# Normalising the first batch's probabilities inside the transposition: a float32 product with a diagonal of reciprocal sums in place of a POOL multiplication

## The chip, the cores and the metric

The kernel runs on one core of a Trainium2 chip. The metric is the device time of one execution in microseconds (us). The engines are named as the profile names them: PE (TensorE matrix products), PEld (its weight loads), DVE (VectorE), ACT (ScalarE), POOL (GpSimd), SP (the engine that starts the loads from memory).

## What is computed

Causal attention with a window of 128 positions and a distance bias, over 8 batches, 8 heads, 576 positions and 64 columns a head; then one feed-forward network over all 4608 rows.

```python
scores = scale * np.matmul(q, k.transpose(0, 1, 3, 2))
...
scores = np.where(mask, scores + bias[None], -1000000000.0)
scores = scores - np.max(scores, axis=-1, keepdims=True)
attn = np.exp(scores)
attn = attn / (np.sum(attn, axis=-1, keepdims=True) + 1e-09)
x = np.matmul(attn, v)            # heads laid side by side: 4608 x 512
...
h = x @ w_in                      # 512 x 2048
g = h * (1.0 / (1.0 + np.exp(-1.702 * h)))
out = g @ w_out                   # 2048 x 512
```

## The kernel before

Attention is done in units: one or two blocks of 128 (or 64) query rows, each against the 128 keys before it and its own. A unit goes through stages, one stage a tick, so that four units are under way at once: `scores` (PE, into `s_ps`, of which there is one buffer), `biased` (DVE adds the bias and takes the row minimum of the negated scores), `exponents` (ACT, with the row sum), `normal` (reciprocal of the sums on DVE, then the multiplication of the probabilities `b.p`, tile `pb`), `flip` (PE transposes the probabilities into `t_ps`, two buffers, which the decoding of weights uses too), `high` (ACT copies them to SBUF, tile `pw` or `ph`), `mix` (PE multiplies by V into `x_ps`), and the copy of the result into `x0` or `xf`, the rows that the network takes.

The first batch is treated otherwise than the rest. Its units are *whole* (`u.whole`): their products with Q, K and V are in plain float32, and their probabilities are multiplied by the reciprocal sums on POOL (L345). There are 24 of them, eight (one a head) for each of the row ranges 0 to 256, 256 to 512 and 512 to 576, called the first, second and third part below. A unit of the first part has two blocks and 3 transposed pieces of 128x128, one of the second two blocks and 4 pieces, one of the third one block of 64 rows and 2 pieces with 64 output columns: 24 + 32 + 16 = 72 pieces. The later batches split every operand into a high and a low float32r part and are normalised on DVE (L349) or ACT (L347); the change does not touch them.

The network works in chunks of 256 rows. For each of the 16 slices `f` of the hidden layer, `up` issues 12 products of 256 columns into `h_ps` (L452), ACT, DVE and POOL form the gate and split it (L457, L458, L461, L462), and `down` issues 6 products of 512 columns into `acc` (L471). The first chunk needs the rows of the first part alone. The weights arrive as raw words and are decoded once, by two operations on ACT (L219, L220), two on DVE (L221, L222), a cast on ACT (L224) and a subtraction on POOL (L225). While the first part is prepared, three products that nobody reads (L197, `spin`) stand behind each tick on PE.

The code issues all this in one program order, ticks between the network's steps by a running credit. A scheduler then orders each engine's instructions by its own estimate of durations; each engine works its list in that order. The loads on SP keep the order of the program. A load of Q or K for a later unit needs one of three raw buffers back, and so waits for the scores of an earlier unit; loads of weights stand behind them on the same queue.

Of the kernel before, what the change touches and what calls it, by code (L numbers as in the profile page):

```python
# [8 lines left out]
F32 = mybir.dt.float32  # L9
# [6 lines left out]
ALU = mybir.AluOpType  # L16
# [5 lines left out]
P = 128  # L22
# [135 lines left out]
def tile_kernel(ctx: ExitStack, tc: tile.TileContext, qT, kT, v, w_in, w_out, out):  # L158
    nc = tc.nc
# [3 lines left out]
    att = ctx.enter_context(tc.tile_pool(name="att", bufs=2))  # L163
# [10 lines left out]
    ident = const.tile([P, P], F32, name="ident")  # L174
# [162 lines left out]
    def normal(u, on_act):  # L337
        u.rec = att.tile([P, 2], F32, name="rec", bufs=3)
        rows, ne = u.blocks[0].rows, len(u.blocks)
        nc.vector.tensor_scalar(u.rec[:rows, :ne], u.sums[:rows, :ne], 1e-9, None, ALU.add)  # L340
        nc.vector.reciprocal(u.rec[:rows, :ne], u.rec[:rows, :ne])
        for e, b in enumerate(u.blocks):
            live = b.p[:rows, b.live:b.end]
            if u.whole:
                nc.gpsimd.tensor_scalar(live, live, u.rec[:rows, e:e + 1], None, ALU.mult)  # L345
            elif on_act:
                nc.scalar.activation(live, live, AF.Copy, scale=u.rec[:rows, e:e + 1])  # L347
            else:
                nc.vector.tensor_scalar(live, live, u.rec[:rows, e:e + 1], None, ALU.mult)  # L349

    def flip(u):

        u.t = ps.tile([P, 4 * P], F32, name="t_ps", bufs=2)
        if u.whole:
            u.ph = u.pl = att.tile([P, 4 * P], F32, name="pw", tag="ph")
        else:
            u.ph = att.tile([P, 4 * P], F32R, name="ph")
            u.pl = att.tile([P, 4 * P], F32R, name="pl")
        u.pspans = []
        w = 0  # L360
        for c in u.chunks:
            start = w
            for b, col in c.parts:
                nc.tensor.transpose(  # L364
                    u.t[:c.n, w:w + b.rows], b.p[:b.rows, col:col + c.n], ident[:b.rows, :b.rows])
                w += b.rows
            c.p = u.ph[:c.n, start:w], u.pl[:c.n, start:w]
            if u.pspans and u.pspans[-1][0] == c.n:
                u.pspans[-1][2] = w
            else:  # L370
                u.pspans.append([c.n, start, w])
# [124 lines left out]
    for b in range(1, B):  # L496
        start = (b * S + S - 1) // T - XBUFS
# [12 lines left out]
    def tick():  # L510

        nonlocal ticks
        n = ticks

        def stage(k, *steps):
            u = units[n + k] if 0 <= n + k < len(units) else None
            for step in steps:
                if u:
                    step(u)

        stage(1, split_q)
        stage(-2, flip, split_v)
        stage(0, lambda u: None if u.whole else load_v(u))
        stage(-1, lambda u: load_v(u) if u.whole else None)
        stage(-1, biased)
        stage(1, split_rest)
        stage(-1, exponents)
        on_act = n - 1 in BESIDE
        if on_act:
            stage(-2, high)  # L530
        stage(-1, lambda u: normal(u, on_act))
        if not on_act:
            stage(-2, high)
        stage(-2, low)
        stage(0, scores)
        stage(-3, mix)
        if n + 1 < len(units) and units[n + 1] and loads:
            load(loads.pop(0))
        ticks += 1
# [121 lines left out]
```

## Time and profile before

| | us |
|---|---|
| median of 3 runs | 1069.25 (1067.49 to 1070.32) |
| the profiled execution | 1072.22 |
| its span, first to last instruction | 1070.4 |
| PE busy over the span | 1054.6 (99%) |
| DVE, ACT, POOL busy | 706.7, 605.4, 636.1 |

The profiled execution took 3.0 us more than the median. Busy time of PE is modelled from overlapping instructions; a PE that is 99% busy says that it hardly ever waits, not that it works at its peak. The first batch's units lie in the first 130 us of the span; from there to the end PE works the network and the later batches. The rows on which the prediction rests stand in it.

### The profile page before, as it was taken

Reading aid. Unit: us, or ns where it says so; the run is one execution under the profiler, and the core shown is the slowest. Engines: PE = TensorE matmul, PEld = TensorE weight load, DVE = VectorE, ACT = ScalarE, POOL = GpSimd, SP = SyncE. Lnnn points to the kernel's source line nnn. Section 1 sums busy time; section 2 is a strip of 40 time slices with the busy share of each in tenths; the row PEclk is TensorE's granted clock in tenths of the full one; section 3 lists DMA queues with packets and bytes.
Section 4 is the critical chain, followed back from the end, with each engine's and each line's share of the span. In section 5 each row is a group of like instructions: output and inputs, shape, how many; then the busy total and the mean of one; then the engine's idle time right before and its main releaser. Section 6 shows DMA issues by size and latency. Waiting matters only on the chain.

```text
span 1070.4 us, 21794 instructions
## 1 busy us (share of the span) xinstructions
PE 1054.6 (99%) x7021; PEld 941.6 (88%) x7021; DVE 706.7 (66%) x2299; ACT 605.4 (57%) x1797; POOL 636.1 (59%) x931
## 2 busy tenths in 40 slices
PE   7999999999999999999999999999999999999998
PEld 4676899998989999999999999999999999998987
DVE  4767898879897777654676668767867687413131
ACT  4797776676766566444555556656565556322222
POOL 3679986667776666544565657656666566323232
PEclk9799999999999999999999999999999999999999
DMA  4974322333322232202222212222222121000000
GB/s 136 305 235 145 83 63 86 105 84 86 86 79 80 60 88 77 61 12 67 63 71 66 62 52 86 72 69 67 85 67 85 52 68 51 9 12 21 1 21 20
DMA packets 97265, 81.24 MB, mean 76 GB/s; under 512 B 50048, under 2 KB 88448, under 8 KB 97152
## 3 DMA queue, kind: packets, MB, share of 16 engines
q1 hardware_dynamic: 91968, 70.42, 23.4%
q10 hardware_dynamic: 5184, 9.44, 2.4%
q8 instruction: 55, 0.90, 0.3%
q14 instruction: 58, 0.48, 0.1%
HBM read 70.39 MB, written 9.44 MB: 75 GB/s over the span
## 4 chain that ended last, share of the span: by engine, by line
PE 93%; DVE 3%; ACT 2%; DMA 1%; issue 1%; POOL 0%; SPq 0%; DVEq 0%; POOLq 0%; ACTq 0%
PE h_ps L452 37%; PE acc L471 37%; PE x_ps L398 5%; PE t_ps L364 5%; PE s_ps L309 5%; PE s_ps L303 1%; PE x_ps L393 1%; PE acc L197 1%; DMA rk<-kT 1%; DMA rw<-w_in 1%; DVE pb L321 1%; ACT pb L332 0%; ACT rw L220 0%; DVE xh L436 0%; SPq L170 0%
## 5 line engine op out<-in xcount | busy, mean ns | idle before, releaser
L452 PE MATMUL h_ps<-xh,w 128*128 128x256 f32 x2304 | 370.1, 284 | 3.6 <-DVE g L458 2.1
L462 POOL TENSOR_TENSOR gl<-g,gh 128x256 fp32r<-128x256 f32 x288 | 215.7, 750 | 255.8 <-ACT gh L461 194.4
L452 PEld LDWEIGHTS h_ps<-xh,w 128*128 128x128 f32 x2304 | 328.2, 188 | 34.7 <-DVE g L458 3.4
L471 PE MATMUL acc<-w,gh 128*128 128x512 f32 x1152 | 325.5, 399 | 0.0
L458 DVE SCALAR_TENSOR_TENSOR g<-g,h_ps 128x256 f32<-128x256 f32 x288 | 119.4, 415 | 180.5 <-ACT g L457 178.9
L457 ACT ACTIVATE g<-h_ps 128x256 f32<-128x256 f32 x288 | 109.6, 381 | 204.1 <-PE h_ps L452 182.5
L471 PEld LDWEIGHTS acc<-w,gh 128*128 128x128 f32 x1152 | 196.0, 188 | 26.9 <-ACT pw L375 0.6
L461 ACT CAST gh<-g 128x256 fp32r<-128x256 f32 x288 | 116.9, 406 | 141.3 <-DVE g L458 129.3
L452 PE MATMUL h_ps<-xl,w 128*128 128x256 f32 x1152 | 194.6, 280 | 0.0
L471 PE MATMUL acc<-w,gl 128*128 128x512 f32 x576 | 188.1, 401 | 0.0
L332 ACT ACTIVATE pb<-pb,mins 128x256 f32<-128x256 f32 (+3 forms) x292 | 141.4, 486 | 58.7 <-DVE mins L321 55.0
L296 POOL TENSOR_TENSOR K<-rk,K 128x384 fp32r<-128x384 f32 (+1 forms) x140 | 126.8, 906 | 77.7 <-ACT Q L276 22.5
L452 PEld LDWEIGHTS h_ps<-xl,w 128*128 128x128 f32 x1152 | 163.3, 188 | 5.5
L321 DVE CUSTOM_DVE_ANT_0 pb<-s_ps,bias 128x256 f32<-128x256 f32 (+5 forms) x320 | 114.6, 377 | 25.3 <-PE s_ps L303 15.5
L295 POOL TENSOR_TENSOR Q<-rq,Q 64x256 fp32r<-64x256 f32 (+1 forms) x140 | 96.4, 689 | 25.3 <-ACT Q L276 5.7
L349 DVE TENSOR_SCALAR pb<-pb,rec 128x256 f32<-128x256 f32 (+2 forms) x252 | 108.5, 467 | 3.3
L364 PE MATMUL t_ps<-ident,pb 128*128 128x128 f32 (+1 forms) x548 | 100.7, 275 | 1.2 <-DVE pl L381 0.6
L471 PEld LDWEIGHTS acc<-w,gl 128*128 128x128 f32 x576 | 92.4, 188 | 8.2 <-POOL pb L345 0.5
L340 DVE TENSOR_SCALAR rec<-sums 128x2 f32<-128x2 f32 (+2 forms) x164 | 51.1, 312 | 61.3 <-ACT pb L332 60.0
L309 PE MATMUL s_ps<-K,Q 128*128 128x256 f32 (+1 forms) x504 | 91.5, 290 | 0.0
L381 DVE TENSOR_TENSOR pl<-t_ps,ph 128x512 fp32r<-128x512 f32 (+2 forms) x140 | 84.1, 603 | 5.4 <-ACT ph L375 5.1
L294 DVE CAST K<-rk 128x384 fp32r<-128x384 f32 (+1 forms) x140 | 57.5, 411 | 34.2 <-PE s_ps L309 30.2
(56 smaller groups left out, 1277.2 us busy)
## 6 DMA issues: line engine op xcount, KB each, us to landing
rk<-kT SPq DMA_DIRECT2D x84, 192.0 KB, 2.6
rq<-qT SPq DMA_DIRECT2D x112, 128.0 KB, 2.5
out<-o ACTq DMA_DIRECT2D x36, 256.0 KB, 2.3
rw<-w_in SPq DMA_DIRECT2D x16, 512.0 KB, 5.2
rw<-w_out SPq DMA_DIRECT2D x16, 512.0 KB, 6.4
rk<-kT SPq DMA_DIRECT2D x56, 128.0 KB, 2.3
rv<-v SPq DMA_DIRECT2D x100, 64.0 KB, 1.9
rq<-qT SPq DMA_DIRECT2D x44, 64.0 KB, 2.2
```

The lines of the kernel that those rows point to most:

```text
L296: nc.gpsimd.tensor_tensor(K2, rk, K1.bitcast(F32), ALU.subtract)
L309: nc.tensor.matmul(u.s[:b.rows, e, b.first:b.end], u.Q[:, b.q0 - u.q0:b.q0 - u.q0 + b.rows], k[:, ko:ko + b.end - b.first], start=(z == 0) ...
L321: nc.vector.tensor_tensor_reduce(b.p[ra:rb, cs:b.end], u.s[ra:rb, e, cs:b.end], bias[head][ra:rb, cs:b.end], -SCALE, BIG, ALU.add, ALU.min ...
L332: nc.scalar.activation(live, live, AF.Exp, bias=u.mins[:b.rows, e:e + 1], scale=-1.0, accum_out=u.sums[:b.rows, e:e + 1],)
L349: nc.vector.tensor_scalar(live, live, u.rec[:rows, e:e + 1], None, ALU.mult)
L364: nc.tensor.transpose(u.t[:c.n, w:w + b.rows], b.p[:b.rows, col:col + c.n], ident[:b.rows, :b.rows])
L452: nc.tensor.matmul(h, w1[f][:, z, k * P:(k + 1) * P], x[:, k], start=(n == 0), stop=(n == len(ops) - 1))
L457: nc.scalar.activation(g, h, AF.Tanh, scale=0.851)
L458: nc.vector.scalar_tensor_tensor(g, g, 1.0, h, ALU.add, ALU.mult)
L461: nc.scalar.copy(gh, g)
L462: nc.gpsimd.tensor_tensor(gl, g, gh.bitcast(F32), ALU.subtract)
L471: nc.tensor.matmul(acc, g[:, t * P:(t + 1) * P], w2[f][:, z], start=(f == self.f0 and n == 0), stop=(f == self.f1 - 1 and n == 2))
```

## The change

For whole units, `normal` no longer multiplies the probabilities on POOL. DVE multiplies the 128x128 identity (64x64 in the third part) by a block's column of reciprocal sums instead, which gives a diagonal matrix, `b.scale`, in a tile that takes its room from the tag `pl` (two buffers; whole units have no `pl` of their own). `flip` then replaces each transposition by a float32 product of the probabilities with that diagonal: the same stationary operand, another moving one, the result transposed and normalised at once. All other units keep their code.

```diff
+        if u.whole:
+            u.scale = att.tile([P, 4 * P], F32, name="scale", tag="pl")
         for e, b in enumerate(u.blocks):
             live = b.p[:rows, b.live:b.end]
             if u.whole:
-                nc.gpsimd.tensor_scalar(live, live, u.rec[:rows, e:e + 1], None, ALU.mult)
+                b.scale = u.scale[:rows, e * P:e * P + rows]
+                nc.vector.tensor_scalar(
+                    b.scale, ident[:rows, :rows], u.rec[:rows, e:e + 1], None, ALU.mult)
...
             for b, col in c.parts:
-                nc.tensor.transpose(
-                    u.t[:c.n, w:w + b.rows], b.p[:b.rows, col:col + c.n], ident[:b.rows, :b.rows])
+                p, to = b.p[:b.rows, col:col + c.n], u.t[:c.n, w:w + b.rows]
+                if u.whole:
+                    nc.tensor.matmul(to, p, b.scale, start=True, stop=True)
+                else:
+                    nc.tensor.transpose(to, p, ident[:b.rows, :b.rows])
```

Line numbers behind `flip` are 7 higher after the change (L452 is L459, L471 is L478, L393 is L400). The scheduler also orders the engines anew, up to the second batch; SP's order stays as it was. Three places matter below.

The first is PE in the first part, at the first two units' transpositions. `t_ps<-ident` is a transposition, `t_ps<-scale` the product in its place, `s_ps` the scores of the fourth unit (u3), `x_ps` the first unit's product with V. Before:

```order
L364 MATMUL t_ps_184<-ident_73,pb_162 128x128
L364 MATMUL t_ps_184<-ident_73,pb_164 128x128 x2
L303 MATMUL s_ps_236<-rk_153,rq_152 128x128
L303 MATMUL s_ps_236<-rk_153,rq_152 128x256
L364 MATMUL t_ps_215<-ident_73,pb_192 128x128
L393 MATMUL x_ps_239<-pw_185,VV_159 64x256
```

and now:

```order
L370 MATMUL t_ps_185<-scale_172,pb_162 128x128
L370 MATMUL t_ps_185<-scale_172,pb_164 128x128 x2
L370 MATMUL t_ps_217<-scale_203,pb_193 128x128
L370 MATMUL t_ps_217<-scale_203,pb_195 128x128 x2
L303 MATMUL s_ps_239<-rk_153,rq_152 128x128
L303 MATMUL s_ps_239<-rk_153,rq_152 128x256
```

Three pieces stood ahead of u3's scores and six products stand there now.

The second is POOL between the first part and the network's first steps, where its multiplications stood among the decoding of weights (`w1`, `w2`, L225) and the splitting of the gate (`gl`, L462). Before:

```order
L345 TENSOR_SCALAR pb_512<-pb_512,rec_520 128x256
L345 TENSOR_SCALAR pb_514<-pb_514,rec_520 128x256
L345 TENSOR_SCALAR pb_648<-pb_648,rec_656 128x256
L345 TENSOR_SCALAR pb_650<-pb_650,rec_656 128x256
L225 TENSOR_TENSOR w1_1_583<-wc_578,w1_1_583 128x512
L225 TENSOR_TENSOR w2_1_592<-wc_587,w2_1_592 128x512
L462 TENSOR_TENSOR gl_570<-g_566,gh_569 128x256
L225 TENSOR_TENSOR w1_2_605<-wc_600,w1_2_605 128x512
```

and now:

```order
L445 TENSOR_TENSOR xl_554<-x0_245,xh_553 128x256
L225 TENSOR_TENSOR w1_1_593<-wc_588,w1_1_593 128x512
L225 TENSOR_TENSOR w2_1_602<-wc_597,w2_1_602 128x512
L225 TENSOR_TENSOR w1_2_615<-wc_610,w1_2_615 128x512
L225 TENSOR_TENSOR w2_2_624<-wc_619,w2_2_624 128x512
L469 TENSOR_TENSOR gl_580<-g_576,gh_579 128x256
```

The decoding of the second pair of weights has nothing of the attention ahead of it any more.

The third is PE in the second part, where transpositions stand among the network's products. Before:

```order
L471 MATMUL acc1_695<-w2_2_614,gh_808 128x512
L364 MATMUL t_ps_724<-ident_73,pb_648 128x128 x2
L364 MATMUL t_ps_724<-ident_73,pb_650 128x128 x2
L364 MATMUL t_ps_758<-ident_73,pb_733 128x128 x2
L364 MATMUL t_ps_758<-ident_73,pb_735 128x128 x2
L471 MATMUL acc0_694<-w2_2_614,gl_809 128x512
```

and now:

```order
L459 MATMUL h_ps_1005<-xh_553,w1_4_723 128x256 x4
L370 MATMUL t_ps_770<-scale_755,pb_744 128x128 x2
L370 MATMUL t_ps_770<-scale_755,pb_746 128x128 x2
L303 MATMUL s_ps_793<-rk_543,rq_542 128x256 x2
L459 MATMUL h_ps_1005<-xh_553,w1_4_723 128x256 x4
```

The pieces stay in PE's list, four to a unit, between products of the network and scores.

## Prediction

> **What bounds the kernel now.** I read the page's busy times and the engines' shares of the chain that ended last, then busy times by stage, then the chain in order of time through the first 130 us, and last the groups of the instructions that the change touches. The page first: busy time of each engine, and the chain's shares.
>
> ```profile
> PE 1054.6 (99%) x7021; PEld 941.6 (88%) x7021; DVE 706.7 (66%) x2299; ACT 605.4 (57%) x1797; POOL 636.1 (59%) x931
> ...
> PE 93%; DVE 3%; ACT 2%; DMA 1%; issue 1%; POOL 0%; SPq 0%; DVEq 0%; POOLq 0%; ACTq 0%
> ```
>
> PE carries the chain, POOL none of it. So a microsecond added to PE where PE is the bound arrives at the end whole, and POOL's time counts only where PE waits for it. Where that is, the stretches of the first batch tell (stretch, length, then busy us of PE, PEld, DVE, ACT, POOL, then granted clock, DMA share, GB/s):
>
> ```profile
> 0.00:24.00 24.00, 19.37 (x102) 12.12 (x102) 9.21 (x47) 8.56 (x28) 9.97 (x20) 1.00 0.42 113
> 24.00:42.00 18.00, 16.71 (x59) 10.19 (x59) 10.99 (x36) 12.22 (x34) 9.56 (x11) 0.62 0.92 280
> 42.00:54.00 12.00, 10.82 (x66) 8.05 (x64) 10.60 (x27) 12.00 (x27) 9.51 (x9) 1.00 1.01 354
> 54.00:105.00 51.00, 48.30 (x276) 35.13 (x276) 35.53 (x115) 44.69 (x115) 42.92 (x45) 1.00 0.64 196
> 105.00:130.00 25.00, 25.00 (x160) 20.49 (x160) 20.63 (x58) 19.04 (x60) 22.84 (x29) 1.00 0.25 67
> ```
>
> Four regimes: to 24 us nothing is full; from 24 to 42 PE is nearly full at a granted clock of 0.62; from 42 to 54 ACT is full (12.00 of 12) with the decoding of weights; from 54 on PE is full but for 2.7 us. The chain in order of time (start, length, what) says what ends each:
>
> ```profile
> 15.80 0.85 PE s_ps L303 x4
> 16.65 0.27 PE t_ps L364
> ...
> 17.84 5.46 DMA rw<-w_in
> 23.37 0.62 ACT w_ps L219
> ...
> 24.57 0.36 ACT pw L375
> ...
> 32.77 0.43 PE t_ps L364 x2
> 33.20 2.00 PE s_ps L303 x4
> ...
> 55.02 1.06 PE s_ps L303 x4
> ...
> 60.74 0.87 PE t_ps L364 x8
> ...
> 65.67 1.01 PE x_ps L393 x6
> ...
> 86.43 0.26 PE t_ps L364 x2
> ...
> 93.26 0.51 PE x_ps L393 x4
> ```
>
> Until 23.4 us everything stands behind the first load of weights: ACT has its decoding (L219) ahead of the copy `pw`, and PE needs that copy.
>
> **The change part by part.** *A product against a transposition.* A float32 product is two records (the scores of the first two parts have 24 products of 256 columns, which show as x48):
>
> ```profile
> L303 PE MATMUL s_ps<-rk,rq 64*128 64x256 f32 x48 | 15.2, 427 | 0.2 <-DVE mins L321 0.2
> ```
>
> A transposition is one. Eight transpositions of 128 columns took 0.87 us, 0.109 each. The nearest products: two of 256 columns (L303 x4) took 1.06 us, so 0.53 each; V's three (L393 x6, of 128, 256 and 128 columns) took 1.01 us, so one of 128 is (1.01 - 0.53) / 2 = 0.24 us. The first part's scores, 128 and 256 columns, took 0.85 us, which would leave 0.32 for the short one, with a weight load in it that nothing hid. Bounds: 0.22 (two transpositions) and 0.32; I take 0.24, since those products follow one another as the new ones will. That is +0.13 us a piece at full clock (bounds 0.11 and 0.21). In the third part two pieces of 64 columns took 0.26 us, two products of 64 columns (L393 x4) 0.51: +0.25 a unit. In all PE gets 56 x 0.13 + 8 x 0.25 = 9.3 us more. What of it reaches the end, by stage:
>
> - To 24 us (12 pieces): the load of `w_in` was issued at 17.84, behind loads that wait for the fifth unit's scores, which ended at 16.65. The new order puts six products (1.44 us) ahead of the fourth unit's scores where three pieces stood; 1.44 - 0.33 = 1.1 us more, of which the wait for DVE's row minima hides about half, so these scores come some 0.6 us later; the fifth unit's come only about 0.2 later, because the pieces that stood between the two have gone ahead. Taken: +0.2 (0 to 0.6).
> - 24 to 42 us (12 pieces, 9 of them at half clock by the timeline): there a piece took 0.43 / 2 = 0.215, twice as much, so a product adds 0.26: 9 x 0.26 + 3 x 0.13 = 2.7 us. PE is on the chain around 33 us, but ACT (12.2 of 18 us) and the DMA (0.92) follow closely, and the exchange of POOL's latency for DVE's shortens the way to the pieces. Taken: +1.5 (0 to 2.7).
> - 42 to 54 us (4 pieces, 0.5 us): PE is idle 1.2 us, ACT is the bound. Taken 0; with that cover gone, 0.5.
> - 54 us on (28 pieces and the 8 units of the third part): 28 x 0.13 + 2.0 = 5.6 us. PE idles 2.7 us here, of which 1.6 is one wait that no transposition is near (below). I let 1 us be filled. Taken: +4.6 (3 to 8, the upper end at 0.21 a piece).
>
> *POOL's multiplications go.* Groups by form (line, engine, operation, shapes, count, then busy us and mean ns):
>
> ```profile
> L345 POOL TENSOR_SCALAR pb<-pb,rec 128x256 f32<-128x256 f32 x24 | 22.1, 929 | 7.7 <-DVE rec L341 4.7 <-ACT w_ps L219 2.3 <-ACT w L224 0.8
> L345 POOL TENSOR_SCALAR pb<-pb,rec 64x192 f32<-64x192 f32 x8 | 6.3, 795 | 0.2 <-DVE rec L341 0.2
> L345 POOL TENSOR_SCALAR pb<-pb,rec 128x128 f32<-128x128 f32 x8 | 4.8, 602 | 17.7 <-DVE rec L341 16.1 <-ACT pb L332 1.0 <-DVE rec L340 0.6
> ```
>
> That is 33.2 us off POOL, which was 84% busy from 54 to 105. What PE waited for there and at 49 us (waits of PE and PEld: for whom, total us, times, longest):
>
> ```profile
> PE h_ps L452 <- POOL w L225: 1.1, 1, 1.1
> PE h_ps L452 <- DVE g L458: 1.6, 1, 1.6
> PEld acc L471 <- POOL pb L345: 0.5, 2, 0.3
> PEld t_ps L364 <- POOL w L225: 0.4, 1, 0.4
> ```
>
> The 1.1 us fell at 49, where POOL subtracted the decoded weights behind two multiplications; but ACT was full there, so at most half counts. With the 0.5, I take -1.0 for all of this (0 to -2.0).
>
> *DVE gets 40 diagonals.* No row shows one. The multiplication of the other batches on DVE, in the same shape, bounds it from above, an operation on one column from below:
>
> ```profile
> L349 DVE TENSOR_SCALAR pb<-pb,rec 128x128 f32<-128x128 f32 x28 | 12.1, 433 | 0.7
> L340 DVE TENSOR_SCALAR rec<-sums 64x1 f32<-64x1 f32 x8 | 1.1, 142 | 0.9 <-ACT pb L332 0.8
> ```
>
> Between 0.14 and 0.43; the same shape is the near one, so 0.43 and 17 us on DVE in all. Two of them (0.86) still come sooner than two multiplications on POOL (1.86). They queue ahead of the next unit's bias, on which its scores wait, and in the ACT stage DVE is at 10.60 of 12. Elsewhere DVE has a third of its time free. Taken: +0.3 (0 to 6, which is the third rival). The room of tag `pl` is not used by whole units, and SP's order is unchanged, so neither costs anything; if the room were short, a diagonal would wait for an earlier unit's products.
>
> Sum: 0.2 + 1.5 + 0 + 4.6 - 1.0 + 0.3 = 5.6 us. From about 140 us on the orders are those of before, and PE is the bound, so nothing makes up for it later. Against the profiled execution of 1072.2 this is 1077.8; that execution stands 3.0 above the median, so against the median of 1069.25 it is 1074.9, and I say 1075.
>
> **The rivals.** *The clock comes back sooner.* The granted clock (the seventh number) was lost after PE had stood still:
>
> ```profile
> 23.00:24.00 1.00, 0.00 (x0) 0.00 (x0) 0.00 (x0) 0.63 (x2) 0.00 (x0) 1.00 0.96 196
> 24.00:25.00 1.00, 0.02 (x1) 0.02 (x1) 0.40 (x1) 1.00 (x3) 0.00 (x0) 0.58 0.92 302
> ...
> 36.00:37.00 1.00, 1.00 (x5) 0.51 (x4) 0.29 (x1) 0.97 (x3) 0.95 (x2) 0.50 0.25 66
> 37.00:38.00 1.00, 1.00 (x5) 0.66 (x3) 0.45 (x2) 0.00 (x0) 0.55 (x1) 0.59 0.69 168
> ```
>
> Half clock from about 24.2 to 37.8, 13.6 us, although PE was busy nearly throughout. With PE fuller, half speed could end earlier or never begin. Each microsecond less of it saves half of one on PE, 6.8 in all, but ACT was idle only 18 - 12.2 = 5.8 us there. Saved 5 of it, the time is 1070: no change. Against it: the wait that brought it on, behind the load of weights, remains. [...]
>
> *POOL was what PE's late inputs hung on (not slower).* POOL was 84% busy from 54 to 105 and stands between the gate's two halves (L462), so units come late in ways that the waits put down to others. The loads of weights on PE show it as short stops from 54 to 130:
>
> ```profile
> PEld x_ps L393 <- issue: 1.6, 6, 0.4
> PEld h_ps L452 <- issue: 1.3, 5, 0.3
> PEld t_ps L364 <- issue: 1.3, 4, 0.4
> PEld s_ps L303 <- issue: 1.0, 5, 0.4
> ```
>
> These 5.2 us and the 2.7 us of idle PE make 7.9. If POOL's relief frees all of it, 5.6 us of new products fit in and 2.3 are won: 0.2 + 1.5 - 2.3 - 1.0 = -1.6, or 1067.7. It decides once more than some 6 us of the 7.9 hang on POOL; the waits that name POOL come to 2.0 in all, which is against it.
>
> *The diagonals come late.* DVE operations that should take 0.3 us took 1.2 beside POOL's subtractions of weights, as the timeline shows:
>
> ```profile
> 27.95 1.27 POOL L225 TENSOR_TENSOR w<-wc,w 128x512 fp32r<-128x512 f32 x1
> ...
> 28.14 1.23 DVE L436 CAST xh<-x 128x256 fp32r<-128x256 f32 x1
> ...
> 38.02 0.29 DVE L436 CAST xh<-x 128x256 fp32r<-128x256 f32 x1
> ```
>
> A diagonal is an operation of the same kind. If one in three of the 16 second- and third-part units is held by 1 us and PE has nothing else in its order, that is 5 to 6 us more: 1081. [...]
>
> **How the numbers follow.** A measurement of this kernel can tell about 0.3%, 3.2 us. The forecast, has 0.60. Its bounds add up to 3 - 2 = 1 and 0.6 + 2.7 + 0.5 + 8 + 0.3 = 12.1 us; all ends of one side will hardly meet, so its own range is 1071 to 1080. Of the others, the clock has 0.14, POOL 0.13, the late diagonals 0.13. The range reaches into the rivals' times on both sides: 1067 to 1081. Slower: 0.52 of the forecast's 0.60 and all of the last, 0.65. Faster by 3.2 us needs two of the gains together, or the clock's with little cost: 0.11. The rest, 0.24, is within.
>
> **What would show it.** Right: L370 as two records a product, 144 in all, and four products at about 0.96 us in the chain; no L345 on POOL, which falls by 33 us; the stage that ended at 54 at nearly the same time, and the rest 4 to 6 us later. The `w_in` load near 18.0. Wrong: products at 0.2 us or less a piece; a granted clock of 1.00 before 34 us; PE's short stops gone from 54 to 105; or PE waiting for L348. The weakest step is how much of the new PE work idle time swallows.

## The result and the profile after

The changed kernel takes 1084.16 us (median of 4 runs, 1078.42 to 1084.92) where the kernel before took 1069.78 beside it (4 runs): a ratio of 1.0116, 95% interval 1.0076 to 1.0156. A second measurement gave 1082.77 (6 runs, 1081.41 to 1086.57) against 1070.05 (17 runs): 1.0126, 1.0085 to 1.0166. The forecast was 1075, its range ended at 1081. It is slower, as forecast, but by 12 to 14 us and not by 5.6.

In the expectations and below, "after" is the changed kernel, and a gain or loss "by the ratio" is the ratio of the runs times 1070 us.

The page of the profiled execution (1084.52 us), busy times and then the chain's shares:

```profile
PE 1064.7 (98%) x7093; PEld 952.3 (88%) x7093; DVE 722.7 (67%) x2339; ACT 607.4 (56%) x1797; POOL 604.4 (56%) x891
...
PE 91%; DVE 5%; ACT 1%; issue 1%; DMA 1%; POOL 0%; SPq 0%; DVEq 0%; POOLq 0%; ACTq 0%
```

POOL fell by 31.7 us, DVE rose by 16.0 and PE by 10.1, with 72 records more. The span rose by 12.3 (1070.4 to 1082.7). So PE's idle time, span less busy, did not fall: 15.8 us before, 18.0 now. This subtraction is the reading that the rest hangs on.

Busy times by stretch, in the columns of the prediction's table, with one more row:

```profile
0.00:24.00 24.00, 20.31 (x119) 13.70 (x120) 12.55 (x62) 10.52 (x32) 2.53 (x10) 1.00 0.46 129
24.00:42.00 18.00, 16.53 (x71) 11.08 (x71) 12.21 (x41) 11.29 (x31) 3.27 (x3) 0.72 0.79 254
42.00:54.00 12.00, 8.50 (x50) 6.38 (x49) 11.26 (x30) 10.84 (x26) 5.04 (x4) 0.96 0.98 345
54.00:105.00 51.00, 50.55 (x292) 38.54 (x291) 36.70 (x112) 40.66 (x99) 24.33 (x24) 0.98 0.60 187
105.00:130.00 25.00, 24.21 (x147) 19.19 (x146) 20.08 (x51) 17.12 (x50) 19.28 (x23) 1.00 0.28 76
130.00:160.00 30.00, 28.48 (x194) 25.02 (x193) 28.01 (x81) 21.47 (x63) 23.99 (x32) 1.00 0.23 63
```

The last row of these in the kernel before:

```profile
130.00:160.00 30.00, 30.00 (x211) 27.57 (x211) 27.50 (x87) 21.37 (x63) 25.44 (x35) 1.00 0.28 74
```

PE's idle time per stretch is length less busy. From 54 to 105 us it fell from 2.70 to 0.45: the products fill it. From 42 to 54 it rose from 1.18 to 3.50, and between 105 and 160, where PE was full before, 0.79 + 1.52 = 2.31 us are new. In the last stretch DVE is at 28.01 of 30.

The chain in order of time (start, length, what) shows the place at 42 to 54 and the price of the products:

```profile
11.65 1.34 PE t_ps L370 x12
...
17.10 4.35 DMA rw<-w_in
...
41.94 4.25 DMA rw<-w_out
...
50.70 0.67 DVE wc L222
51.36 0.80 DVE scale L348 x2
52.17 0.61 DVE w_ps L221
52.77 0.33 DVE g L465
53.10 0.04 issue
53.15 2.93 PE h_ps L459 x12
56.08 1.14 PE t_ps L370 x8
...
63.89 0.89 PE t_ps L370 x8
...
114.11 0.62 PE t_ps L370 x4
```

In the list of PE's waits from 42 to 54 us it is one wait (for whom, total us, times, longest):

```profile
PE h_ps L459 <- DVE g L465: 3.0, 1, 3.0
```

PE stands for 3.0 us, from 50.16 on, before the network's products `h_ps`, which need the buffer that DVE's gate step `g` gives back. For the first 1.2 us ACT's part of the gate (L464) was not done, since ACT works on decoding ahead of it; for the rest DVE is not at `g` yet, behind decoding (L221, L222) and two diagonals. The timeline of POOL, DVE and ACT there (start, length, operation, what it waited for):

```profile
48.49 1.27 POOL L225 TENSOR_TENSOR w<-wc,w 128x512 fp32r<-128x512 f32 x1 [3.64 <-ACT w L224]
48.90 0.89 DVE L340 TENSOR_SCALAR rec<-sums 128x2 f32<-128x2 f32 x1
...
50.62 1.27 POOL L225 TENSOR_TENSOR w<-wc,w 128x512 fp32r<-128x512 f32 x1 [0.86 <-ACT w L224]
51.01 0.64 ACT L464 ACTIVATE g<-h_ps 128x256 f32<-128x256 f32 x2
51.29 0.68 DVE L348 TENSOR_SCALAR scale<-ident,rec 128x128 f32<-128x128 f32 x1
...
52.69 0.73 DVE L465 SCALAR_TENSOR_TENSOR g<-g,h_ps 128x256 f32<-128x256 f32 x2
```

Two operations of DVE took longer than usual and ended with a subtraction of POOL: `rec` 0.89 us, where the median of the first 130 us is 0.16, and the first of the two diagonals 0.68, where the median of all 40 is 0.28. Together that is 1.1 us. In the kernel before, `g` stood right behind DVE's copy into `xf`, with no decoding between:

```profile
48.03 0.41 DVE L427 COPY xf<-x_ps 64x256 f32<-64x256 f32 x1
48.36 0.40 DVE L458 SCALAR_TENSOR_TENSOR g<-g,h_ps 128x256 f32<-128x256 f32 x1
```

Now that copy (L434) starts at 50.38, and L222, the diagonals and L221 stand between it and `g`. When PE goes on, it is at half clock:

```profile
50.00:51.00 1.00, 0.15 (x2) 0.00 (x0) 1.00 (x4) 1.00 (x3) 0.38 (x1) 1.00 1.02 397
...
53.00:54.00 1.00, 0.85 (x4) 0.85 (x5) 1.00 (x4) 1.00 (x4) 1.00 (x1) 0.53 1.01 406
54.00:55.00 1.00, 1.00 (x6) 1.00 (x6) 0.90 (x3) 1.00 (x3) 1.00 (x3) 0.50 0.99 389
```

### The profile page after: what moved, and what is told of

Read it like the earlier page. It is cut to its first block, busy times and chain, and to the rows that moved or that the text cites. A ratio compares the mean times of both kernels' runs of the same rounds, so it can differ in the third digit from the quotient of the medians.

```text
span 1082.7 us, 21916 instructions
## 1 busy us (share of the span) xinstructions
PE 1064.7 (98%) x7093; PEld 952.3 (88%) x7093; DVE 722.7 (67%) x2339; ACT 607.4 (56%) x1797; POOL 604.4 (56%) x891
## 3 DMA queue, kind: packets, MB, share of 16 engines
q1 hardware_dynamic: 91968, 70.42, 22.9%
## 4 chain that ended last, share of the span: by engine, by line
PE 91%; DVE 5%; ACT 1%; issue 1%; DMA 1%; POOL 0%; SPq 0%; DVEq 0%; POOLq 0%; ACTq 0%
PE h_ps L459 36%; PE acc L478 36%; PE x_ps L405 5%; PE s_ps L309 5%; PE t_ps L372 4%; PE t_ps L370 2%; PE s_ps L303 1%; PE x_ps L400 1%; PE acc L197 1%; DVE pb L321 1%; DVE w_ps L221 1%; DVE xh L443 0%; DVE pb L353 0%; DVE wc L222 0%; DVE g L465 0%
## 5 line engine op out<-in xcount | busy, mean ns | idle before, releaser
L459 PE MATMUL h_ps<-xh,w 128*128 128x256 f32 x2304 | 370.6, 284 | 6.7 <-DVE g L465 4.6
L459 PEld LDWEIGHTS h_ps<-xh,w 128*128 128x128 f32 x2304 | 328.3, 189 | 36.6 <-DVE g L465 6.8
L478 PE MATMUL acc<-w,gh 128*128 128x512 f32 x1152 | 325.8, 400 | 0.7 <-ACT gh L468 0.7
L464 ACT ACTIVATE g<-h_ps 128x256 f32<-128x256 f32 x288 | 109.7, 382 | 204.1 <-PE h_ps L459 189.0
L478 PEld LDWEIGHTS acc<-w,gh 128*128 128x128 f32 x1152 | 195.8, 188 | 27.8 <-ACT gh L468 1.2
L459 PE MATMUL h_ps<-xl,w 128*128 128x256 f32 x1152 | 196.0, 281 | 0.0
L478 PE MATMUL acc<-w,gl 128*128 128x512 f32 x576 | 188.2, 401 | 0.0
L459 PEld LDWEIGHTS h_ps<-xl,w 128*128 128x128 f32 x1152 | 164.3, 188 | 6.0 <-DVE xl L445 0.2
L478 PEld LDWEIGHTS acc<-w,gl 128*128 128x128 f32 x576 | 92.7, 188 | 8.8 <-issue 0.8
L372 PE MATMUL t_ps<-ident,pb 128*128 128x128 f32 x476 | 87.0, 273 | 1.2 <-DVE pl L388 0.6
```

What stands on the lines that cost most here:

```text
L372: nc.tensor.transpose(to, p, ident[:b.rows, :b.rows])
L459: nc.tensor.matmul(h, w1[f][:, z, k * P:(k + 1) * P], x[:, k], start=(n == 0), stop=(n == len(ops) - 1))
L464: nc.scalar.activation(g, h, AF.Tanh, scale=0.851)
L478: nc.tensor.matmul(acc, g[:, t * P:(t + 1) * P], w2[f][:, z], start=(f == self.f0 and n == 0), stop=(f == self.f1 - 1 and n == 2))
```

## The experiments

The first four do a part of the change, or a variant of it, in the order that the scheduler then makes. The next seven hold an order fixed: the instructions are edited in each engine's finished list, so that every engine works the list of another kernel; the changed kernel was run again beside the last of them. The final two try the clock. For each profile I give PE's idle time.

**Products only.** Before, with a product with the plain identity instead of each transposition; POOL keeps its work.

```diff
-                nc.tensor.transpose(
-                    u.t[:c.n, w:w + b.rows], b.p[:b.rows, col:col + c.n], ident[:b.rows, :b.rows])
+                p, to = b.p[:b.rows, col:col + c.n], u.t[:c.n, w:w + b.rows]
+                if u.whole:
+                    nc.tensor.matmul(to, p, ident[:b.rows, :b.rows], start=True, stop=True)
```

> Plain identity as moving operand: the whole units' transpositions become float32 products, POOL still multiplies, DVE gets no diagonals. Theory D (DVE: its 16 us of diagonals came where DVE had no room, and cost 6 to 9 of the 12 to 14 us; the products cost some 5): 4 to 7 us over before. Theory P (PE: the 144 records themselves cost nearly all): 10 to 14 us over. Theory S (the new order of instructions costs it, whatever was moved): anything, with no relation to the sum.

Measured: 1080.64 us against 1072.04, ratio 1.0078 (1.0054 to 1.0103), 8.4 us. This lies between the 4 to 7 us and the 10 to 14 us of the two theories that had a figure. The profile has no half-clock stretch in its first 240 us, and its four runs had mean granted clocks of 0.998 and 0.999, so it is not the clock. Idle time is 18.7 us, and it lies where it had not been expected (below them the last row in the kernel before):

```profile
130.00:160.00 30.00, 26.50 (x182) 23.49 (x182) 27.62 (x88) 22.37 (x69) 23.97 (x34) 1.00 0.32 84
240.00:400.00 160.00, 154.94 (x1059) 141.59 (x1058) 131.40 (x443) 101.47 (x313) 108.30 (x168) 0.99 0.29 80
...
240.00:400.00 160.00, 158.21 (x1093) 144.64 (x1092) 131.33 (x450) 102.47 (x320) 110.67 (x174) 1.00 0.29 80
```

PE misses 3.5 us after the first batch is done, with DVE nearly full, and between 240 and 400 us 5.1, which is 3.3 more than before. No product in place of a transposition stands there; something else had moved.

**No normalisation on POOL.** Before without L345, with nothing in its place.

```diff
             if u.whole:
-                nc.gpsimd.tensor_scalar(live, live, u.rec[:rows, e:e + 1], None, ALU.mult)
+                pass
```

> Transpositions as before, POOL's 40 multiplications left out, nothing in their place: the whole units' probabilities stay unnormalised. D and P: POOL's relief is worth 0 to 2 us, so 1067.5 to 1070. S: several us to either side. If POOL was what PE's late inputs hung on: 4 us or more faster.

Measured: 1073.78 (1068.46 to 1082.95) against 1072.04, ratio 1.002 (0.9988 to 1.0051). Inconclusive: mean granted clocks ran from 0.983 to 0.996, and the times follow them.

**Diagonals only.** Transpositions stay, POOL's multiplication is left out, DVE makes the 40 diagonals, which nobody reads.

```diff
-                nc.gpsimd.tensor_scalar(live, live, u.rec[:rows, e:e + 1], None, ALU.mult)
+                b.scale = u.scale[:rows, e * P:e * P + rows]
+                nc.vector.tensor_scalar(
+                    b.scale, ident[:rows, :rows], u.rec[:rows, e:e + 1], None, ALU.mult)
```

> Transpositions as before, POOL's multiplications left out, DVE makes the 40 diagonals and nobody reads them: the probabilities stay unnormalised. D: 5 to 9 us over e2_no_norm. P: within 2 us of e2_no_norm.

Measured: 1080.93, ratio 1.0078 (1.0053 to 1.0103), 8.4 us, some 7 us over the run without POOL's work. Its mean granted clocks are low, 0.985 to 0.992 where before's median beside it is 0.995, but the run at 0.992 took 1080.32 us, as long as that at 0.985 (1080.14), so the clock alone does not explain it. In 42 to 54 us DVE is full and PE idles 4 us:

```profile
42.00:54.00 12.00, 7.93 (x45) 5.42 (x43) 11.90 (x31) 10.29 (x25) 3.83 (x3) 1.00 1.04 348
```

**The change, with the diagonals on POOL.**

```diff
-                nc.vector.tensor_scalar(
+                nc.gpsimd.tensor_scalar(
                     b.scale, ident[:rows, :rows], u.rec[:rows, e:e + 1], None, ALU.mult)
```

> As the change, with the 40 diagonals made on POOL (128x128 instead of POOL's former 128x256). D: PE's part is left, 4 to 7 us over before. P: 10 to 14 us over, as the change.

Measured: 1078.3, ratio 1.006 (1.0035 to 1.0084), 6.4 us. PE is busy 10.91 of 12 us from 42 to 54, so DVE's diagonals had a part in the wait there; from 130 to 160 it is busy 26.53 of 30, as with products only. Products alone cost 8.4, diagonals alone 8.4, the whole 12 to 14: the parts don't add, and what they have in common is a new order of everything.

**Before's order, products.** The order is made with transpositions; then the 72 become products.

```diff
+    for f in nc.m.functions:
+        for block in f.blocks:
+            for i, x in enumerate(block.instructions):
+                if x.name in SWAP:
+                    block.instructions[i] = copy.replace(x, is_transpose=False)
```

> The kernel before, ordered by the scheduler with its 72 transpositions of whole units, which are turned into float32 products with the same identity after the ordering: the order of every engine is that of before, only the 72 operations differ. e1_product_only did the same operations in an order made for products, and lay 8.5 us over before. Theory P (the products' own time on PE, 9.3 us by the sum): 8 to 11 us over before at an equal granted clock. Theory S (the order that the scheduler makes when it sees products lets DVE become the bound from 125 to 150 us): 2 to 5 us over.

Measured: 1074.94 against 1071.93, ratio 1.0025 (1.001 to 1.0039), 2.7 us. Page and stretches:

```profile
PE 1060.7 (99%) x7093; PEld 950.3 (89%) x7093; DVE 708.4 (66%) x2299; ACT 606.9 (57%) x1797; POOL 634.7 (59%) x931
...
24.00:42.00 18.00, 17.55 (x100) 12.23 (x99) 13.44 (x51) 15.60 (x42) 11.68 (x14) 1.00 1.06 311
42.00:54.00 12.00, 11.09 (x68) 8.70 (x66) 9.64 (x21) 12.00 (x28) 10.41 (x11) 1.00 1.04 361
...
130.00:160.00 30.00, 30.00 (x211) 27.41 (x210) 27.55 (x81) 20.65 (x61) 24.59 (x34) 1.00 0.30 78
```

With a span of 1073.5 PE idles 12.8 us, 3.0 less than before: here the products do fill waits, as the forecast had it, and the third part of 8.4 us is left.

**The order of "products only", transpositions.** The reverse: the order is made with products, then they are turned back.

```diff
-                    block.instructions[i] = copy.replace(x, is_transpose=False)
+                    block.instructions[i] = copy.replace(x, is_transpose=True)
```

> The converse: the order of e1_product_only, with its 72 products turned back into transpositions after the ordering. P: as before, within 2 us at an equal granted clock. S: 4 to 7 us over before, with DVE full and PE waiting between 125 and 150 us.

Measured: 1081.97 (1077.91 to 1084.81), ratio 1.0092 (1.0061 to 1.0122), 9.8 us for an order alone, above the 4 to 7 expected; idle 22.9 us. Its stretches:

```profile
120.00:135.00 15.00, 13.30 (x90) 11.37 (x89) 14.81 (x43) 12.39 (x34) 14.28 (x19) 1.00 0.39 103
135.00:150.00 15.00, 12.15 (x80) 10.41 (x81) 14.56 (x47) 10.32 (x31) 11.42 (x17) 1.00 0.29 74
...
165.00:180.00 15.00, 15.00 (x105) 13.78 (x104) 8.70 (x30) 7.10 (x22) 7.56 (x11) 1.00 0.27 80
```

and the same of before:

```profile
120.00:135.00 15.00, 15.00 (x99) 12.75 (x98) 13.70 (x37) 12.13 (x35) 14.47 (x18) 1.00 0.30 79
135.00:150.00 15.00, 15.00 (x106) 13.74 (x106) 13.84 (x45) 11.67 (x33) 13.03 (x20) 1.00 0.25 63
...
165.00:180.00 15.00, 15.00 (x104) 13.71 (x103) 12.12 (x40) 9.53 (x30) 9.79 (x14) 1.00 0.27 74
```

DVE is at 98% between 120 and 150 us, PE starves for 4.5 us, and from 165 on DVE has 3.4 us less to do than before: work that PE did not need yet was put early on the engine that PE waits for. This run too idles more between 240 and 400 us (4.6 us, before 1.8).

**The whole change in another order.** The scheduler sees transpositions that read the diagonals; afterwards they become products, so every operation is that of the change.

```diff
+                    piece = nc.tensor.transpose(to, p, b.scale)
+                    SWAP.add(getattr(piece, "ins", piece).name)
```

> All operations of the change, in an order that the scheduler made while it took the 72 products for transpositions (they are turned into products after the ordering). P: as the change, 10 to 14 us over before. S: 3 to 7 us over before, clearly under the change.

Measured: 1076.89 (1075.97 to 1078.89), ratio 1.0053 (1.0035 to 1.0072), 5.7 us: the same work with a different order is about half as dear. The operations are those of the change, and PE waits for the diagonals here too, so nothing but the order differs. PE is full from 105 to 150 us; the wait at 42 to 54 stays (PE 8.48 of 12).

**The work of the change in before's order**, in three steps, each part also by itself. Behind each reciprocal a multiplication of the diagonal's size is put into DVE's list; POOL's is cut to one column.

```diff
+        if products and x.name in SWAP:
+            x = copy.replace(x, is_transpose=False)
+        if cut and x.name in NORM:
+            x = copy.replace(x, ins=(one(x.ins[0]), x.ins[1]), outs=(one(x.outs[0]),))
...
+        if diagonals and x.opcode == "Reciprocal" and x.outs[0].memref in scale:
+            for e, m in enumerate(scale[x.outs[0].memref]):
...
+                out.append(copy.replace(
+                    m, name=f"I-9{n:04d}", engine=x.engine,
...
```

> The kernel before in its own order, with nothing but 40 diagonal-sized VectorE multiplications added behind the reciprocals, read by nobody. Theory S: 0 to 3 us over before, since VectorE has idle time from 20 to 42 us and little of the 11 to 16 us meets a TensorE that waits. Theory D: 6 to 11 us over before, as in the run that had the diagonals and a new order (1080.9).

> The kernel before in its own order, with POOL's 40 multiplications cut to one column (probabilities unnormalised). The forecast's term for POOL's relief: 1.0 us under before, with a bound of 0 to 3. If POOL was what TensorE's late inputs hung on (the rival at 1067.7), 5 to 7 us under before.

> All the work of the change, put into the order that every engine has before: the 72 transpositions become products, 40 diagonal-sized VectorE multiplications are issued right behind their reciprocals (nobody reads them; the products read the plain identity), and POOL's 40 multiplications are cut to one column, so the probabilities stay unnormalised. It leaves out TensorE's wait for the diagonal. Theory S (what the forecast missed is the new order): with the order kept, the time is near the forecast, 1073 to 1077 us, and PE stays full at 105 to 160 us. Theory D (the diagonals fill VectorE whatever the order): 1080 to 1085, with VectorE at 97% or more of 42 to 54 us and of 120 to 150 us.

Measured, all against 1072.26: diagonals 1074.29, ratio 1.0019 (0.9995 to 1.0044), 2.0 us, an interval that holds zero; POOL's work cut 1069.37, 0.997 (0.9958 to 0.9983), -3.2 us; all of it 1077.19 (1076.23 to 1078.07), 1.0039 (1.0024 to 1.0053), 4.2 us, with 2.6 to 5.7 as its interval. The forecast of 5.6 lies in it. All of it, page and stretch:

```profile
PE 1061.9 (99%) x7093; PEld 951.2 (88%) x7093; DVE 719.5 (67%) x2339; ACT 607.5 (56%) x1797; POOL 613.4 (57%) x931
...
42.00:54.00 12.00, 10.81 (x69) 8.79 (x70) 11.20 (x28) 11.77 (x27) 7.22 (x8) 1.00 1.06 330
...
130.00:160.00 30.00, 30.00 (x207) 27.23 (x208) 27.55 (x85) 22.51 (x65) 25.56 (x35) 1.00 0.25 64
```

The diagonals are there, and neither the wait at 42 to 54 nor the loss after 130 is: PE idles 14.4 us (span 1076.3). That the forecast of 5.6 is met is in part luck: in this profile PE's work rose by 7.3 us and its idle time fell by 1.4, where the sum had 10.5 and 4.9 (worked out below). Two things flatter the 4.2. At an equal mean clock of 0.995 this kernel took 1077.56 and 1078.07, some 6 us over before's median of 1071.6 in ten runs. And PE's wait for the diagonal itself is not in this kernel; the changed kernel's trace puts one short wait of the products down to a diagonal (L348), 0.3 us. On the other side POOL is busy 9 us longer than in the changed kernel (613.4 and 604.4), with its cut operations.

**The changed kernel's own order, without its products**, and the changed kernel beside it.

```diff
+                    plain = copy.replace(ident, ap=[[ident.ap[0][0], rows], [1, n]])
+                    block.instructions[i] = copy.replace(x, is_transpose=True, ins=(plain, x.ins[1]))
```

> Every engine's order is that of the changed kernel, with its 40 diagonals and without POOL's multiplications, but the 72 products are turned back into transpositions with the plain identity once the order stands (probabilities unnormalised). In the order of before, the diagonals cost 2.0 us and POOL's work was worth 3.2, so by the work alone this kernel would be 1 us under before. Theory S (the changed kernel's own order costs): 5 to 9 us over before, with PE short of work at 42 to 54 us and VectorE at 95% or more of 130 to 160 us, as in the changed kernel; the rest up to the changed kernel's time is the products. Theory P (the products cost most, in whatever order): within 2 us of before.

> The changed kernel itself on the same chip as the run before it, for the difference between the two: 1080 to 1085 us, 10 to 14 us over before; over a1 by 3 to 6 us if the 72 products cost about what the forecast put on them (6.3 us with those at half clock, 4.6 from 54 us on), by 10 us or more under theory P.

Measured against 1070.05: 1078.56 (1071.33 to 1081.82, 12 runs), ratio 1.006 (1.0031 to 1.0089), 6.4 us, with the changed kernel at 13.5. Six of the twelve runs had a mean granted clock of 0.989 (1078.96 to 1081.82 us), two had 0.998 (1071.33 and 1072.24). Where the clocks agree, at 0.997, before has 1066.32 to 1070.81 with a median of 1068.98 (5 runs), this kernel 1072.97 (one run) and the changed kernel 1081.41 and 1081.63: about 4 us for the order and 8.5 for the products in it. Here "the order" has the diagonals in it, and PE's waits for them. The expected 95% of DVE from 130 to 160 us did not come (27.21 of 30, and PE idles 1.1 us there). Page of this kernel, and its wait from 42 to 60 us (its lines are numbered 3 higher than the changed kernel's):

```profile
PE 1053.9 (98%) x7021; PEld 941.6 (88%) x7021; DVE 722.8 (67%) x2339; ACT 606.9 (57%) x1797; POOL 603.0 (56%) x891
...
PE h_ps L462 <- DVE g L468: 3.0, 1, 3.0
```

The wait of 3.0 us stands there without a product on PE, and again in the second profile of the changed kernel. That profile lost no clock before 48 us, so it can be laid beside before's order with products, which lost none either. Its page and stretches:

```profile
PE 1061.5 (98%) x7093; PEld 950.7 (88%) x7093; DVE 723.9 (67%) x2339; ACT 607.6 (56%) x1797; POOL 604.0 (56%) x891
...
24.00:42.00 18.00, 15.56 (x87) 10.84 (x88) 14.63 (x51) 15.07 (x40) 4.54 (x4) 1.00 1.04 300
42.00:54.00 12.00, 8.97 (x51) 7.95 (x52) 9.51 (x22) 9.60 (x22) 6.83 (x7) 0.86 1.04 359
...
130.00:160.00 30.00, 28.19 (x189) 24.88 (x188) 27.68 (x79) 21.79 (x64) 24.18 (x33) 1.00 0.25 64
```

Idle from 24 to 54 us: 2.44 + 3.03 = 5.5 here, 0.45 + 0.91 = 1.4 there; from 130 to 160: 1.8 and 0. That is 5.9 us, and the spans differ by 6.1 (1079.6 and 1073.5). Over the whole span idle time differs by 5.3 us (18.1 and 12.8), as some is won back from 54 to 105, and PE's work by 0.8.

**Ten more spin pairs**, to keep PE busy where it waits 2.15 us at 22.8 in the kernel before. In the first try they stood one mixing too late, at 36 us, where PE did not wait.

```diff
+            for _ in range(pairs):
+                n += 1
+                extra += [copy.replace(load, name=f"I-9{2 * n:05d}", sync_info=None),
+                          copy.replace(out[k], name=f"I-9{2 * n + 1:05d}", sync_info=None)]
+            out[at:at] = extra
```

> The kernel before in its own order, with ten more spin pairs (bf16 products of the identity that nobody reads, 0.2 us each) on TensorE in the 2.1 us in which it waits at 22.8 to 25.0 us, just ahead of the half-clock stretch of 24 to 38 us. If the loss of the clock follows that gap and costs what the times against the granted clock say (0.9 to 1 us for each 0.001 of mean clock), the clock stays at 1.00 until 42 us, the mean is 0.998 or more in every run, and the time is 1 to 4 us under before. If the stage is held by ACT and VectorE so that the clock doesn't matter there, the clock rises and the time stays within 1 us. If the gap is not what loses the clock, the half-clock stretch stays.

> The ten extra spin pairs of the run before, now at the right place: in the kernel before's own order, between the score products that end at 22.8 us and the x_ps product that starts at 24.98 us, where TensorE waits 2.15 us for ScalarE's copy (in the run before they stood one mixing later, at 36 us, where TensorE did not wait). If gaps of over 2 us are what loses the clock (in the profiles so far every one of the seven gaps of 2.15 us and more is followed by half clock, and of nine of 0.9 to 1.5 us two are), the clock stays at 1.00 from 20 to 42 us and the time is 1 to 3 us under before. If the loss hangs on something else, the half-clock stretch appears as often and the time stays within 1 us.

Measured: misplaced 1071.14 against 1072.26, ratio 0.9996 (0.9977 to 1.0015), its profile with the gap (2.29 us) and the half clock behind it; in the gap 1070.29 against 1070.55, ratio 0.9999 (0.9982 to 1.0017). The profile of the latter has full clock through the place:

```profile
23.00:24.00 1.00, 1.00 (x11) 0.71 (x8) 0.79 (x2) 1.00 (x5) 0.00 (x0) 1.00 1.05 226
24.00:25.00 1.00, 1.00 (x7) 0.65 (x7) 0.97 (x6) 1.00 (x3) 0.00 (x0) 1.00 0.98 372
```

None of its 12 runs fell under a clock of 0.995, of the 17 beside it 5 did, but the time did not move. The expectation of 1 to 3 us failed, and no version here that still normalises beats the kernel before.

## Why the prediction was wrong, step by step

**What it got right.** The price of the products: on the chain six of 128 columns (x12) took 1.34 us and four (x8) mostly 0.89, which is 0.22 a piece and the lower bound, but twice 1.09; two of 64 columns (x4) took 0.62, where 0.51 was said. The work on PE, forecast at 9.3 us and 1.2 more for half clock, shows as 10.1 on the page. POOL fell by 31.7 (33 said), L370 has 144 records, the first load of weights started at 17.10 (18.0 said). Four of the 28 pieces that the sum put behind 54 us started at 53.4 in the kernel before, which moves 0.5 us from one term to another. The diagonals took 0.40 us a piece (DVE's 16.0 us over 40), 0.43 said, which is luck: the median is 0.28, and 11 of them took 0.45 to 1.30.

**The step that failed** is the price of the order, which the sum put at nothing: "0" for 42 to 54, the term from 54 us on, which lets waits be filled and none arise, and the sentence that from about 140 us on the orders are those of before "and PE is the bound". I read the new order at three places and took PE's idle time elsewhere as given. The first of the three did no harm: the load of `w_in` started 0.7 us earlier than before, not 0.2 later, and PE's idle time to 24 us fell by 0.9. The sum of 5.6 holds 10.5 us of PE time, and so it has PE's waits shortened by 4.9 in all. In the profile the waits grew by 2.2. The gap between the two, 7.1 us, is nearly the miss of the profiled pair (12.3 less 5.6). By stretch, idle time was to fall by 1.2 from 24 to 42 us, by 0.5 from 42 to 54 and by 1.0 behind that, POOL's relief aside; it rose by 0.2, rose by 2.3, and fell by 2.3 to 105 but rose by as much again to 160. Put into before's order, the same work costs 4.2 us (2.6 to 5.7), in the scheduler's order 12 to 14; all operations of the change in a third order 5.7; and the changed kernel's order, diagonals included, costs 6.4 us (3.3 to 9.5) with no product in it. That the order costs this much is shown, not argued.

**Its places.** At 42 to 54 I let ACT be the bound, with 0.5 us as the worst. PE waited 3.0 us, 1.2 of them for ACT and the rest for DVE. It takes both, the diagonals on DVE and the scheduler's order around them: in the five profiles of the four kernels that have the diagonals on DVE and an order made for them, PE waits 3.0 to 3.5 us at one time for `g`, and in none of the other eleven profiles does it wait over 1.6 at one time between 42 and 60 us. PE's busy time says the same less sharply: 7.93 to 8.97 of 12 in the five, 10.12 and 10.81 with diagonals in before's order, 10.70 in the order of "products only", 10.91 with the diagonals on POOL, though also 9.88 with POOL's work cut. From 105 to 160 PE lost 2.3 us, 1.9 of them to DVE's row minima and `g`, and no rival had it; that DVE does later work too early there, as in the order of "products only", is not shown for this kernel.

**The late diagonals** are the rival that came nearest. Eleven of the 40 were held beside an operation of POOL and ended within 0.1 us of it, nine of them in nine of the 16 units of the second and third part, by 0.2 to 1.1 us each. Its condition was met, but PE mostly had other work: from 54 to 105 us it idled 0.45 us in all. At 42 to 54 the diagonal and `rec` together were held for 1.1 of the 3.0 us, as DVE had hardly a pause ahead of `g`; the rival's 5 to 6 us are not in the trace.

**The other rivals.** That the clock comes back sooner is true of the products in before's order (ten runs at a mean granted clock of 0.996 to 1.000, where 14 of the 17 runs of before beside them had 0.990 to 0.996): part of why they cost 2.7 us and not 6 (at a clock of 0.998 six of those ten took 1074.65 to 1075.25 us, and two of before 1067.90 and 1069.19). In the changed kernel half clock stands again at the end of the new wait, for 3.40 us from 53 us on. The miss is not the clock's: the changed kernel's one run at 1.000 took 1078.42 us, and two of before at 0.999 took 1065.88 and 1067.17. Whether products keep the clock better than transpositions is not settled: an order with transpositions also kept full clock (POOL's work cut: no slow stretch in its profile, which has a mean clock of 1.000). That POOL was what held PE is wrong: its work is worth 3.2 us (1.8 to 4.5) in before's order, over my 1.0 and under the 5 to 7 that the rival needs, and in the profile even that is not a shorter wait: PE idles 17.7 us, 1.9 more than before, and its work is 5.7 us less with no stretch at half clock.

**What stays open** is how the 12 to 14 us of the changed kernel divide between waits and clock: by all runs the order is 6.4 and the products 7, at a clock of 0.997 some 4 and 8.5, from one run of the kernel between. How much of the order's price hangs on the diagonals that it has to place on DVE is open too.

## What to carry to other kernels

Where a scheduler orders the engines by its own estimates, a change of one operation's cost is two changes: the work, and a new order of everything. Price the second by itself: compare PE's idle time (span less busy) before and after, and run the new operations in the old order, or the old ones in the new. A forecast that lets waits be filled must name who is waited for in the new order, not in the old one.

## What the runs showed of the hardware

The 22 half-clock stretches in the first 240 us of sixteen profiles lasted about 3.41 us or a multiple of it: 12 of them 3.40 to 3.42 us, five 6.82 to 6.84, two 10.24, two 13.66 and one 30.72 (summed from rows of 1 us). Over the 99 runs of the kernel before that stood beside the experiments, the time is 0.9 us longer for each 0.001 that the mean granted clock is lower (the slope of a line through them). In the first 60 us of these profiles, from PE's first product on, PE stood still ten times for 2.15 to 4.45 us, and each time half clock began before its end or at most 1.5 us behind it; of 17 gaps of 0.9 to 1.93 us it followed three. But a stretch also came behind a gap of no more than 0.81 us (at 11 us in the whole change in before's order), and filling the one gap kept the clock in one profile and did not move the time, so what loses the clock is not settled.

Diagonals on DVE took longer beside operations of POOL: of the 40 in the changed kernel, 29 took 0.24 to 0.29 us, and the 11 others, at 0.45 to 1.30, all ended within 0.1 us behind an operation of POOL.
